# The first batch in quarters, and two PSUM banks in one tile

## The chip, the cores and the metric

The kernel runs on one core of one Trainium2 chip. Its engines are TensorE (PE; its weight loads are listed as PEld), VectorE (DVE), ScalarE (ACT), GpSimd (POOL) and SyncE (SP), each with a queue of its own that is worked off in order. The metric is the device time of one execution in microseconds (us).

## The reference

For each of 8 batches and 8 heads, 576 queries of 64 elements attend to 72 keys and values, each the mean of 8 neighbouring rows. The attention's output, as 4608 tokens of 512 elements, goes through four experts, whose outputs are summed with weights from `domain_probs`.

```python
k_p = k.reshape(B, H, Sp, pool, D).mean(axis=3)      # Sp = 72, pool = 8
v_p = v.reshape(B, H, Sp, pool, D).mean(axis=3)
attn = softmax(scale * q @ k_p.transpose(0, 1, 3, 2))
x = (attn @ v_p).transpose(0, 2, 1, 3).reshape(B * S, H * D)
p = domain_probs / (domain_probs.sum(-1, keepdims=True) + 1e-09)
for e in range(E):                                   # E = 4
    h = np.maximum(x @ w1[e], 0.0)                   # 512 -> 1024
    out += p[:, e:e + 1] * (h @ w2[e])               # 1024 -> 512
```

## The kernel before

**Work and order.** Tokens are worked in nine chunks of 512: chunk c below 8 holds the first 512 queries of batch c, chunk 8 the 64 that remain of each batch. All arithmetic on matrices is in bf16 with sums in f32. The instructions stand on every engine in the order in which the Python code calls them; nothing is rescheduled. The framework adds the semaphore waits: it works out, from the tiles that an instruction reads and writes, which earlier instructions it has to wait for.

**The loop.** From chunk 1 on, an expert's two matrix products are each done as seven block products (a Strassen form: sums of blocks of the weights, of x and of the hidden values replace an eighth product). A step `g` of the loop issues one up product of unit 0 (step `i`), one of unit 1 (the step before) and one down product of the expert before (`down`, line 766), so an expert takes seven steps and the 32 experts of chunks 1 to 8 take 224. In each step, TensorE does 4 + 4 + 8 matmuls of 256 columns.

- An up product (`up_product`, L698) goes to a bank of its unit, and ScalarE or VectorE reads it: a copy in step 0 (L711), copies to `partial` in steps 2 and 3 (L713), relus on ScalarE in steps 1 and 5 (L715, L719), relu sums on VectorE in steps 4 and 6 (L678).
- A down product goes to one of the two `o_ps` banks, in turns. After step 0 ScalarE copies it to the other bank (L774). Otherwise it is added into `acc` in two halves: by VectorE (`add`, L845), by ScalarE where an expert 0 writes first (L843), or by ScalarE and GpSimd together in step 4 (L778, L780).
- VectorE also makes four sums of hidden values for an expert (`hidden_sums`, L250), the sums of x (`x_sum`), and `weight_sums` in the first steps of the loop.
- The attention of the next batch is put between the steps, by slots of a plan (28 steps for a batch). Scores of two pairs are issued in one slot by `scores_of_two`: the first pair into `att`, the second into the second banks of both units; ScalarE's exponentials (L399, L413) read them. In the step after it, the two up products are issued in reverse. Contexts (L463) are divided on VectorE (L424, L425), and turned by DMA transposes on SP's queue, as keys and queries are.

**PSUM.** There are eight banks of 512 f32 columns. `att` is one tile of two banks. Unit 1 has two tiles of one bank, `o_ps` has two tiles of one bank, and the last two banks belong to `att_first` in the first batch, then to unit 0 as two tiles.

```python
units = [None, [psum.tile([P, NT], F32, name=f"unit1{i}") for i in range(2)]]
chains = [psum.tile([P, NT], F32, name=f"o_ps{i}") for i in range(2)]
```

**Chunk 0** is done before the loop, up to 65.2 us. `attention_first` does the attention of batch 0 and most of expert 0's up products, while the weights are still loading. Keys and values are pooled by matmuls: `sum_pool` (L314) multiplies the raw rows by a 0/1 matrix `takes`, two heads at a time; the pooled keys are copied twice side by side (L323), and turned by TensorE (`keys`, L304 and L306). Scores (L543) and exponentials (L547) run in four pieces: head group 0 or 1 by token half 0 or 1. Contexts then run by 128 tokens, the first of them in two halves of the heads (`context_half`, L437; `turn_half`, L452), the others whole (L463, L481), and `up_first` (L634) issues up products of 128 columns between them, with relus at L640. The rest of expert 0 follows in `up` (L617, relu at L622).

`first_chunk` then does plain up products of expert 1, block products of experts 2 and 3, the seven down steps of expert 0, and `down_plain` (L792: eight matmuls of 512 columns, added by VectorE at L845) for experts 1 and 2, four times each, in alternate `o_ps` banks. The attention of batch 1 is put between them: its folds (L275, L293), its queries (L371, L374), keys, scores and contexts. At the end, `down_last` (L825) does the last expert's down products in the banks of both units and of `o_ps`.

Of the kernel before, what the change touches and what calls it, by code (L numbers as in the profile page):

```python
# [12 lines left out]
BF16 = mybir.dt.bfloat16  # L13
# [4 lines left out]
def kernel(  # L18
# [44 lines left out]


    att = psum.tile([P, 2, NT], F32, name="att")
    units = [None, [psum.tile([P, NT], F32, name=f"unit1{i}") for i in range(2)]]
    chains = [psum.tile([P, NT], F32, name=f"o_ps{i}") for i in range(2)]
    psum_first = tc.tile_pool(name="psum_first", bufs=1, space=bass.MemoryType.PSUM)
    att_first = [att, psum_first.__enter__().tile([P, 2, NT], F32, name="att_first")]

# [224 lines left out]
    def keys(b, hs):  # L295
        state[("kpT", b)] = kpTs[b % 3]
        if b >= BUSY:
            nc.sync.dma_start_transpose(
                out=state[("kpT", b)][:, 0:H], in_=kp_all[:].rearrange("j h a d -> j (h a d)")
            )  # L300
            return
        kpt_ps = (chains[1][:] if b else spare_bank()).bitcast(BF16)[:, 0:H * SP].rearrange("p (h j) -> p h j", j=SP)
        for h in range(hs.start, hs.stop):
            nc.tensor.transpose(kpt_ps[:, h, :], kp_all[0:SP, h], ident[:SP, :SP])  # L304
        copy = nc.scalar.copy if b else nc.vector.tensor_copy
        copy(out=state[("kpT", b)][:, hs, 0:SP], in_=kpt_ps[:, hs])  # L306

    def sum_pool(nm, g, banks):
        n = 2 * D
# [7 lines left out]
            h = 4 * g + 2 * half  # L317
            yield slice(h, h + 2), banks[half].rearrange("j (h d) -> j h d", d=D)

    def sum_keys(g, banks):  # L320
        copies = (nc.scalar.copy if g else nc.vector.tensor_copy, nc.scalar.copy)
        for copy, (hs, kp) in zip(copies, sum_pool("kraw", g, banks), strict=True):
            copy(out=kp_all[0:SP, hs], in_=kp.unsqueeze(2).to_broadcast([SP, 2, 2, D]))  # L323

    def sum_values(g, banks):
        for hs, vp in sum_pool("vraw", g, banks):
            nc.vector.tensor_copy(out=vps[0][:, hs, 0:D], in_=vp)

    def idle(n, w_ps=None, cols=NT):

# [96 lines left out]
            in1=inv.unsqueeze(3).to_broadcast([P, n, NPAIR, D]), op=ALU.mult,  # L427
        )

    def context_half(r, g, bank):  # L430

        if g == 0:
            state[("x", 0, r)] = npool.tile([P, 2, NPAIR, D], BF16, name="x_tok", bufs=4)
        c_ps = bank.rearrange("p (a n) -> p a n", a=1)
        for i in range(NPAIR):
            at = i * (D + 1)
            nc.tensor.matmul(  # L437
                c_ps[:, 0, at:at + D + 1],
                lhsT=state[("expT", 0)][:, g * NPAIR + i, r // 2, r % 2, :],
                rhs=vps[0][:, g * NPAIR + i, :], skip_group_check=True,  # L440
            )
        divide(c_ps, state[("x", 0, r)][:, g:g + 1])

    def turn_half(r, g, bank):
        if ("xT", 0) not in state:
            state[("xT", 0)] = xpool.tile([P, KC, NT], BF16, name="xT")
        x_tok = state[("x", 0, r)][:].rearrange("p a h d -> p (a h d)")
        ks = slice(g * HK, (g + 1) * HK)
        xt_ps = bank.bitcast(BF16)[:, 0:HK * P].rearrange("p (k t) -> p k t", t=P)
        for i in range(HK):  # L450
            kc = g * HK + i
            nc.tensor.transpose(xt_ps[:, i, :], x_tok[:, kc * P:(kc + 1) * P], ident[:])  # L452
        copy = nc.scalar.copy if g else nc.vector.tensor_copy
        copy(out=state[("xT", 0)][:, ks, r * P:(r + 1) * P], in_=xt_ps)

    def context(b, r, c_ps=None):
        expT, vp = state[("expT", b)], vps[b % 3]
# [13 lines left out]
    def turn(b, r):  # L471
        if ("xT", b) not in state:
            state[("xT", b)] = xpool.tile([P, KC, NT], BF16, name="xT")
        x_tok = state.pop(("x", b, r))[:].rearrange("p a h d -> p (a h d)")
        dst = state[("xT", b)][:, :, r * P:(r + 1) * P]
        if b >= BUSY:
            nc.sync.dma_start_transpose(out=dst, in_=x_tok)
            return
        xt_ps = (units[1][0][:] if b else att_first[1][:, 0] if r == 3 else chains[0][:]).bitcast(BF16)[:, 0:KC * P].rearrange("p (k t) -> p k t", t=P)
        for kc in range(KC):  # L480
            nc.tensor.transpose(xt_ps[:, kc, :], x_tok[:, kc * P:(kc + 1) * P], ident[:])  # L481
        copy = nc.vector.tensor_copy if b == 0 and r == 3 else nc.scalar.copy
        copy(out=dst, in_=xt_ps)

    def rem_queries(i):
        qTr = apool.tile([P, NPAIR, 2, REM], BF16, name="qTr")
# [65 lines left out]
    def attention_first():  # L552

        lo, hi = groups(0)
        first, second, third, fourth = (slice(r * P, (r + 1) * P) for r in range(NR))
        half = slice(HN, NT)
        idle(13)
        rows_chosen(0)
        round_q(0)
        round_q(1)  # L560
        rows_chosen(1)
        queries(0, 0)
        queries(0, 1)
        idle(1)
        queries(0, 2)
        queries(0, 3)
        work, (B2, A2) = units[1], att_first
        work = [work[0][:], work[1][:]]
        sum_keys(0, work)
        idle(3, A2[:, 0], P)  # L570
        sum_keys(1, [B2[:, 0], B2[:, 1]])
        keys(0, lo)
        scores_first(0, 0, A2)
        keys(0, hi)
        sum_values(0, work)
        scores_first(1, 0, B2)
        context_half(0, 0, chains[1][:])
        scores_first(0, 1, A2)
        sum_values(1, work)
        turn_half(0, 0, chains[1][:])  # L580
        scores_first(1, 1, B2)
        context_half(0, 1, chains[0][:])
        context(0, 1, A2)
        up_first(range(0, 2), first, range(0, HK))
        turn_half(0, 1, chains[0][:])
        context(0, 2, B2)
        up_first(range(2, 4), first, range(0, HK))
        turn(0, 1)
        up_first(range(0, 4), first, range(HK, KC))
        context(0, 3, A2)  # L590
        turn(0, 2)
        up_first(range(0, 4), second)
        turn(0, 3)
        up_first(range(0, 4), third)
        up_first(range(0, 4), fourth)
        up_first(range(4, FCH), first)
        up_first(range(4, FCH), second)
        up(0, 0, range(4, FCH), half)

# [20 lines left out]
            nc.scalar.activation(  # L622
                out=dst, in_=out_ps.rearrange("p (t n) -> p t n", n=HN), func=ACT.Relu)

    def up_first(fcs, at, kcs=range(KC)):

        xT, H_sb = x_of(0), hidden[(0, 0)]
        for fc in fcs[::2]:
            if kcs.start == 0:
                state[("up", fc)] = (units[1] + chains[1:])[turn_of("up", 3)][:, 0:2 * P]  # L630
            out_ps = state[("up", fc)]
            for i in range(2):
                for kc in kcs:
                    nc.tensor.matmul(  # L634
                        out_ps[:, i * P:(i + 1) * P],
                        lhsT=w1_bf[:, 0, kc, (fc + i) * P:(fc + i + 1) * P], rhs=xT[:, kc, at],
                        start=(i == 0 and kc == 0), stop=(kc == KC - 1), skip_group_check=True,
                    )
            if kcs.stop == KC:
                nc.scalar.activation(  # L640
                    out=H_sb[:, fc // HF, at.start // HN, fc % HF:fc % HF + 2, at.start % HN:at.start % HN + P],
                    in_=out_ps.rearrange("p (i n) -> p i n", n=P), func=ACT.Relu)

    def weight_parts(e):
        w = w1_bf[:, e]
# [321 lines left out]
    def pieces_later():  # L967
# [17 lines left out]
            q=6, k=(5, 8, 11, 14), v=(13, 16, 19, 26), x=(24, 25, 25, 25), rem=(0, 7, 8, 14),  # L985
        )
        plans[B] = dict(usual, x=(24, 24, 25, 25), rem=(-3, 17, 21, 22))
        plans[BUSY + 1] = dict(usual, keys=-8, values=4, v=(5, 8, 12, 16))

        for b, plan in plans.items():  # L990
            start = 7 * E * (b - BUSY)
# [11 lines left out]
            if b < B:  # L1003
                put(start + plan["queries"], lambda b=b: queries(b))
                put(start + plan["keys"], lambda b=b: fold_keys(b))
                put(start + plan["keys"] + (b > BUSY), lambda b=b: keys(b, every))
                put(start + plan["values"], *values_folds(b))
                pair = 0
                for slot, n in plan["scores"]:
                    if n == 2:  # L1010
                        put(start + slot, lambda b=b, pair=pair: scores_of_two(b, pair))
                        put_amid(start + slot + 1, lambda b=b, pair=pair: scores(b, pair, 1))
                    else:
                        put(start + slot, lambda b=b, pair=pair: scores(b, pair))
                    pair += n

                for r, slot in zip((2, 3, 0, 1), plan["contexts"]):
                    put(start + slot, lambda b=b, r=r: context(b, r))
                    put(start + slot + 1, lambda b=b, r=r: turn(b, r))
# [13 lines left out]
    with tc.manual_schedule(  # L1033
# [29 lines left out]
        later, amid = pieces_later()  # L1063
        below_of = [(0, 3)] + order
        sums = {}
        for at, pieces in (((3,), weight_sums(3)[3:]), ((10, 11, 11, 12), weight_sums(1)), ((10, 15, 22, 14), weight_sums(2))):
            for slot, piece in zip(at, pieces, strict=True):
                sums.setdefault(slot, []).append(piece)
        POOLED = (4,)
# [55 lines left out]
```

## Time and profile before

| | |
|---|---|
| median of 3 runs | 489.67 us (489.37 to 489.85) |
| the profiled execution | 489.64 us, of which the span from first to last instruction is 487.80 |
| TensorE busy | 480.9 us (99% of the span) |
| VectorE, ScalarE, GpSimd busy | 378.3, 305.6, 120.7 us |
| TensorE clock granted | full in every slice |
| first plain up product of expert 1 | 23.23 us |
| first up product of the loop | 65.26 us |

The page's first part gives the busy time of each engine, the second divides the span into 40 slices, and the fourth follows the chain of work that ended last back from the end: what stands in it set the time, what does not was hidden. In a timeline, a line gives the start and the duration of one or more instructions of a kind, the engine, the source line, output and input tiles; a bracket at the end tells how long the engine had been idle and what it waited for. Matmuls are pipelined: eight of 256 columns that "took 1.04" give way to the next one 0.87 after their start.

### The profile page before, as it was taken

The numbers are of one execution on the slowest core, as the hardware profiler recorded it, in microseconds if no ns is written. First come the engines' busy times: TensorE is split into PE (matmuls) and PEld (weight loads), VectorE is DVE, ScalarE is ACT, GpSimd is POOL, SyncE is SP. The second block draws the span as 40 slices with busy tenths as digits, with TensorE's granted clock in tenths as the row PEclk, the third lists the DMA queues.
The fourth block names the chain that finished last, engine by engine and source line by source line (L and its number), as shares of the span: only waits on it lengthen the run. The fifth ranks groups of instructions, "written<-read, shape, count | busy, mean of one in ns | idle before, by whom it ended". The sixth has DMA issues, their size and how long they took to land.

```text
span 487.8 us, 11611 instructions
## 1 busy us (share of the span) xinstructions
PE 480.9 (99%) x4717; PEld 412.3 (85%) x4721; DVE 378.3 (78%) x763; ACT 305.6 (63%) x584; POOL 120.7 (25%) x121
## 2 busy tenths in 40 slices
PE   8999999999999999999999999999999999999996
PEld 4868578898889888888889889888888888888885
DVE  5789799899768976797679866997678766876674
ACT  5887446855676567656765567556765566556650
POOL 8440504243523154016411352111011101010000
PEclk9999999999999999999999999999999999999999
DMA  9999999886876789345945297311112010004003
GB/s 200 207 209 203 203 183 142 98 90 52 99 113 58 88 88 134 36 82 55 163 49 90 26 159 73 69 23 65 36 23 23 23 66 3 12 23 86 1 1 88
DMA packets 102981, 41.98 MB, mean 86 GB/s; under 512 B 73984, under 2 KB 102400, under 8 KB 102928
## 3 DMA queue, kind: packets, MB, share of 16 engines
q0 software_dynamic: 58064, 22.42, 41.0%
q1 hardware_dynamic: 43744, 17.77, 17.3%
q10 hardware_dynamic: 1120, 1.05, 0.6%
q8 instruction: 37, 0.61, 0.5%
q14 instruction: 16, 0.13, 0.1%
HBM read 45.69 MB, written 9.44 MB: 113 GB/s over the span
## 4 chain that ended last, share of the span: by engine, by line
PE 95%; POOL 1%; DMA 1%; ACT 1%; issue 0%; DVE 0%; POOLq 0%
PE unit L698 42%; PE o_ps L766 41%; PE o_ps L792 3%; PE att L463 2%; DMA w_bf<-in_moe_w_dram 1%; PE unit L825 1%; POOL wt_bf L144 1%; PE o_ps L617 1%; PE att L388 1%; PE unit L617 1%; PE unit L634 1%; PE unit L388 1%; ACT qT L374 0%; PE o_ps L634 0%; PE att L517 0%; PE att L500 0%
## 5 line engine op out<-in xcount | busy, mean ns | idle before, releaser
L845 DVE SCALAR_TENSOR_TENSOR acc<-o_ps,p_all,acc 128x256 f32<-128x256 f32 (+1 forms) x285 | 127.0, 486 | 51.5 <-PE o_ps L766 36.0
L766 PEld LDWEIGHTS <-H 128*128 128x128 bf16 x1320 | 129.1, 98 | 15.1
L698 PEld LDWEIGHTS <-w_bf 128*128 128x128 bf16 x1088 | 105.2, 98 | 13.4 <-issue 0.6
L678 DVE CUSTOM_DVE_ANT_0 H<-unit,partial 128x512 bf16<-128x512 f32 x128 | 87.3, 685 | 24.8 <-PE unit L698 10.9
L766 PE MATMUL o_ps<-w_bf,H 128*128 128x256 bf16 x792 | 102.6, 273 | 0.0
L698 PE MATMUL unit<-xT,w_bf 128*128 128x256 bf16 x704 | 100.4, 273 | 0.0
L780 POOL TENSOR_TENSOR acc<-acc,addend 128x512 f32<-128x512 f32 x24 | 30.7, 1277 | 252.3 <-ACT addend L778 211.7
L713 ACT COPY partial<-unit 128x512 f32<-128x512 f32 x128 | 72.3, 592 | 30.3 <-PE unit L698 30.2
L698 PEld LDWEIGHTS <-wu_bf 128*128 128x128 bf16 x816 | 77.6, 98 | 11.6 <-issue 2.5
L698 PE MATMUL unit<-xs,wu_bf 128*128 128x256 bf16 x512 | 77.0, 273 | 0.0
L766 PE MATMUL o_ps<-wt_bf,H 128*128 128x256 bf16 x528 | 68.4, 273 | 0.0
L715 ACT ACTIVATE H<-unit 128x512 bf16<-128x512 f32 x66 | 39.9, 605 | 30.7 <-PE unit L698 30.7
L766 PEld LDWEIGHTS <-S 128*128 128x128 bf16 x528 | 51.7, 98 | 6.0
L719 ACT ACTIVATE H<-unit 128x512 bf16<-128x512 f32 x66 | 39.6, 602 | 25.6 <-PE unit L698 25.3
L711 ACT COPY unit<-unit 128x512 f32<-128x512 f32 x68 | 39.3, 581 | 25.1 <-PE unit L698 18.6
L698 PE MATMUL unit<-xs,w_bf 128*128 128x256 bf16 x256 | 38.4, 273 | 0.0
L154 POOL DMA_DIRECT2D kraw<-in_k_dram x20 | 26.4, 1320 | 39.6 <-DMA kraw<-in_k_dram 39.6
L843 ACT ACTIVATE acc<-o_ps,p_all 128x256 f32<-128x256 f32 x72 | 30.7, 485 | 8.8 <-PE o_ps L766 7.2
L698 PE MATMUL unit<-xT,wu_bf 128*128 128x256 bf16 x240 | 35.7, 272 | 0.0
L766 PE MATMUL o_ps<-w_bf,S 128*128 128x256 bf16 x264 | 34.2, 273 | 0.0
L766 PE MATMUL o_ps<-wt_bf,S 128*128 128x256 bf16 x264 | 34.2, 273 | 0.0
L154 POOL DMA_DIRECT2D vraw<-in_v_dram x20 | 28.6, 1430 | 20.1 <-DMA vraw<-in_v_dram 20.1
(157 smaller groups left out, 508.9 us busy)
## 6 DMA issues: line engine op xcount, KB each, us to landing
out_dram<-acc SPq DMA_DIRECT2D x32, 256.0 KB, 4.3
w_bf<-in_moe_w_dram POOLq DMA_DIRECT2D x11, 512.0 KB, 12.8
q_sb<-in_q_dram POOLq DMA_DIRECT2D x7, 512.0 KB, 10.0
vraw<-in_v_dram POOLq DMA_DIRECT2D x22, 144.0 KB, 6.5
kraw<-in_k_dram POOLq DMA_DIRECT2D x21, 144.0 KB, 5.7
w_bf<-in_moe_w_dram POOLq DMA_DIRECT2D x2, 1024.0 KB, 13.9
wt_bf<-in_k_dram POOLq DMA_DIRECT2D x4, 144.0 KB, 5.4
wt_bf<-in_v_dram POOLq DMA_DIRECT2D x4, 144.0 KB, 4.1
```

Of the source, the lines that this page charges most:

```text
L154: nc.gpsimd.dma_start(out=raw[:], in_=rows_of(src, b, 2 * part, 2 * part + 2), accum_op=ALU.add if part else ALU.bypass)
L678: nc.vector._custom_dve(TENSOR_ADD_SAT, out=dst, in0=ps, in1=part, s0=LARGEST, s1=0.0)
L698: nc.tensor.matmul(ps[:, n * HN:(n + 1) * HN], lhsT=lhs[:, kc, f:f + P], rhs=rhs[:, kc, :], start=(not grows and n == 0 and kc == 0), stop ...
L711: nc.scalar.copy(out=banks[1][:], in_=ps)
L713: nc.scalar.copy(out=part[:, step - 2], in_=ps)
L715: nc.scalar.activation(out=quarter(0, 0), in_=ps, func=ACT.Relu)
L719: nc.scalar.activation(out=quarter(0, 1), in_=ps, func=ACT.Relu)
L766: nc.tensor.matmul(ps[:, j], lhsT=lhs[:, i, j * P:(j + 1) * P], rhs=rhs[:, i, :], start=(not grows and i == 0 and j == 0), stop=(i == HF - 1),
L780: nc.gpsimd.tensor_add(out=dst, in0=dst, in1=addend[:])
L792: nc.tensor.matmul(o_ps, lhsT=lhs, rhs=w2_bf[:, e, fc, :], start=(fc == 0), stop=(fc == FCH - 1), skip_group_check=True,)
L843: nc.scalar.activation(out=dst, in_=o_ps, func=ACT.Copy, scale=prob)
L845: nc.vector.scalar_tensor_tensor(out=dst, in0=o_ps, scalar=prob, in1=dst, op0=ALU.mult, op1=ALU.add,)
```

## The change

- `unit1` becomes one tile of two banks, and `o_ps` too; `units[1][i]` and `chains[i]` are now views of one bank in them. All other code uses the views as before.
- `sum_keys` makes the pooled keys in turned form: the raw rows are now the stationary operand and `takes` the moving one, one head at a time (36 matmuls of 72 columns for a group of four heads, in place of 18 of 128 columns and four turnings). One copy that spans both banks then writes four heads, and a second one writes the lower half of the rows of `kpT`.
- Contexts, turnings and up products of batch 0 run in quarters: four heads by 256 tokens (`context_quarter`, `turn_quarter`, `up_quarter`, with matmuls of 256 columns). The second half of expert 0's up products is then done over all 512 tokens in four products.
- The order of `attention_first` is rewritten around that; the other values are copied by ScalarE in part.
- In the plan of batch 3, the turning of the keys moves from slot -7 to slot -6; two of the four weight sums of expert 1 move by one step each.

```diff
-    units = [None, [psum.tile([P, NT], F32, name=f"unit1{i}") for i in range(2)]]
-    chains = [psum.tile([P, NT], F32, name=f"o_ps{i}") for i in range(2)]
+    unit_banks = psum.tile([P, 2, NT], F32, name="unit1")
+    units = [None, [unit_banks[:, i] for i in range(2)]]
+    chain_banks = psum.tile([P, 2, NT], F32, name="o_ps")
+    chains = [chain_banks[:, i] for i in range(2)]
...
-    def sum_keys(g, banks):
-        copies = (nc.scalar.copy if g else nc.vector.tensor_copy, nc.scalar.copy)
-        for copy, (hs, kp) in zip(copies, sum_pool("kraw", g, banks), strict=True):
-            copy(out=kp_all[0:SP, hs], in_=kp.unsqueeze(2).to_broadcast([SP, 2, 2, D]))
+    def sum_keys(g, banks, copies):
+        for r in range(ROWS):
+            for hh in range(2):
+                for half in range(2):
+                    ps = slice(half * PR, (half + 1) * PR)
+                    nc.tensor.matmul(
+                        banks[0:D, half, hh * SP:(hh + 1) * SP], lhsT=raws[("kraw", 0)][ps, g, hh, r, :],
+                        rhs=takes[ps, r], start=(r == hh == 0), stop=(r == ROWS - 1), skip_group_check=True,
+                    )
+        kpT = state[("kpT", 0)] = kpTs[0]
+        for dup, copy in enumerate(copies):
+            copy(out=kpT[dup * D:(dup + 1) * D, 4 * g:4 * g + 4, 0:SP].rearrange("p (b h) j -> p b h j", b=2),
+                 in_=banks[0:D, :, 0:2 * SP].rearrange("p b (h j) -> p b h j", j=SP))
...
+    def up_quarter(t, g, banks, pairs=range(2)):
         xT, H_sb = x_of(0), hidden[(0, 0)]
+        at = slice(t * HN, (t + 1) * HN)
+        for pair in pairs:
             for i in range(2):
+                f = (2 * pair + i) * P
+                for kc in range(g * HK, (g + 1) * HK):
                     nc.tensor.matmul(
+                        banks[pair][:, i * HN:(i + 1) * HN], lhsT=w1_bf[:, 0, kc, f:f + P], rhs=xT[:, kc, at],
+                        start=(i == kc == 0), stop=(kc == KC - 1), skip_group_check=True,
                     )
+            if g:
                 nc.scalar.activation(
+                    out=H_sb[:, 0, t, 2 * pair:2 * pair + 2, :].rearrange("p i n -> p (i n)"),
+                    in_=banks[pair], func=ACT.Relu)
...
+        (B2, A2), C2 = att_first, chain_banks
+        work, tail = [bank[:] for bank in units[1]], chains
+        vector, scalar = nc.vector.tensor_copy, nc.scalar.copy
+        sum_keys(0, unit_banks, (vector, scalar))
+        idle(3, B2[:, 0], P)
         scores_first(0, 0, A2)
+        sum_keys(1, unit_banks, (vector, vector))
+        scores_first(0, 1, B2)
+        scores_first(1, 0, A2)
+        sum_values(0, work, (vector, vector))
         scores_first(1, 1, B2)
+        context_quarter(0, 0, C2)
+        context_quarter(1, 0, A2)
+        sum_values(1, work, (vector, scalar))
+        turn_quarter(0, 0, tail[1], scalar)
+        turn_quarter(1, 0, A2[:, 0], scalar)
+        up_quarter(0, 0, tail, (0,))
+        context_quarter(0, 1, B2)
+        up_quarter(0, 0, tail, (1,))
+        up_quarter(1, 0, work, (0,))
+        context_quarter(1, 1, A2)
+        up_quarter(1, 0, work, (1,))
+        turn_quarter(0, 1, B2[:, 0], scalar)
+        up_quarter(0, 1, tail)
+        turn_quarter(1, 1, A2[:, 0], scalar)
+        up_quarter(1, 1, work)
+        for fc, bank in enumerate((tail + work), HF):
+            up(0, 0, (fc,), bank=bank)
...
-        plans[BUSY + 1] = dict(usual, keys=-8, values=4, v=(5, 8, 12, 16))
+        plans[BUSY + 1] = dict(usual, keys=-8, turned=-6, values=4, v=(5, 8, 12, 16))
...
-        for at, pieces in (((3,), weight_sums(3)[3:]), ((10, 11, 11, 12), weight_sums(1)), ((10, 15, 22, 14), weight_sums(2))):
+        for at, pieces in (((3,), weight_sums(3)[3:]), ((10, 10, 11, 11), weight_sums(1)), ((10, 15, 22, 14), weight_sums(2))):
```

## The prediction

> **What bounds the kernel now.** I read the page's busy table and clock row first, then its chain, then the timeline of a steady stretch, then of the front.
>
> ```profile
> PE 480.9 (99%) x4717; PEld 412.3 (85%) x4721; DVE 378.3 (78%) x763; ACT 305.6 (63%) x584; POOL 120.7 (25%) x121
> PEclk9999999999999999999999999999999999999999
> PE 95%; POOL 1%; DMA 1%; ACT 1%; issue 0%; DVE 0%; POOLq 0%
> PE unit L698 42%; PE o_ps L766 41%; PE o_ps L792 3%; PE att L463 2%; DMA w_bf<-in_moe_w_dram 1%; PE unit L825 1%; POOL wt_bf L144 1%; PE o_ps L617 1%; PE att L388 1%; PE unit L617 1%; PE unit L634 1%; PE unit L388 1%; ACT qT L374 0%; PE o_ps L634 0%; PE att L517 0%; PE att L500 0%
> ```
>
> TensorE is the bound and hardly ever waits: 95% of the chain is its matmuls, at full clock. So a stall of TensorE is paid in full, and what other engines save is worth nothing. The next view is the timeline of the loop: start, duration, engine, line.
>
> ```profile
> 266.66 0.60 PE L698 MATMUL unit<-xs,wu_bf 128*128 128x256 bf16 x4
> 267.10 1.04 PE L766 MATMUL o_ps<-wt_bf,S 128*128 128x256 bf16 x8
> 267.97 0.60 PE L698 MATMUL unit<-xs,wu_bf 128*128 128x256 bf16 x4
> 268.17 0.88 DVE L845 SCALAR_TENSOR_TENSOR acc<-o_ps,p_all,acc 128x256 f32<-128x256 f32 x2 [0.20 <-PE o_ps L766]
> 268.41 0.60 PE L698 MATMUL unit<-xT,w_bf 128*128 128x256 bf16 x4
> 268.85 1.04 PE L766 MATMUL o_ps<-wt_bf,H 128*128 128x256 bf16 x8
> ...
> 271.73 0.84 ACT L778 ACTIVATE addend<-o_ps,p_all 128x256 f32<-128x256 f32 x2 [0.77 <-PE o_ps L766]
> ```
>
> A step is two up products (0.44 each) and one down product (267.10 to 267.97: 0.87), 1.75 us. The two adds that read the down product start 0.20 after it (0.27 elsewhere) and end at 269.05. The next down product starts at 268.85, before that: it writes the other o_ps bank. The kernel lives on this overlap.
>
> **The waits, the main term.** The change makes one tile of the two o_ps banks, and one of the two banks of unit 1. I followed the semaphore waits of both built programs back to the instruction that each names. Before, all 197 waits of a matmul for a reader of o_ps name a reader of the bank it will write. After, 205 of 240 name a reader of the other bank; so do 175 of the 259 on unit 1. Each down product must now wait until the previous one is read out. Queued behind that wait are all later matmuls.
>
> The price of a step: adds end 0.20 to 0.27 (take 0.235) + 0.87 after the product; restart of TensorE 0.06 (below: 9.68 + 0.31 to 10.05); together 1.16, of which the up products cover 0.87: a stall of 0.29. Where ScalarE reads (0.84), 0.20 + 0.84 + 0.06 - 0.87 = 0.22. After down step 0 it is 0.20 + 0.57 (the L774 copy) + 0.06 < 0.87: none. After down step 6 the adds also stand behind a hidden sum and a relu sum (0.68 each, L250 and L678) that were queued after the adds of step 5: I get 0.33. An expert of seven down steps: 4 x 0.29 + 0.22 + 0.33 = 1.71; an expert 0, whose steps 1, 2, 3 and 6 are read by ScalarE, 4 x 0.22 + 2 x 0.29 = 1.46. The loop has 24 and 8 of them: 41.0 + 11.7 = **52.7**.
>
> **Scores in the loop.** In five of six batches at slot 2, in all six at slot 9, scores go to the second banks of both units. The next step is issued in reverse, unit 1 first, into the other bank; now it waits for the second exponential.
>
> ```profile
> 291.65 0.38 PE L388 MATMUL unit<-qT,kpT 64*128 64x256 bf16 x4
> 291.97 0.61 PE L698 MATMUL unit<-xs,wu_bf 128*128 128x256 bf16 x4
> 292.31 1.07 ACT L413 ACTIVATE expT<-unit 72x512 bf16<-72x512 f32 x2
> ```
>
> 0.20 + 1.07 + 0.06 = 1.33, against 0.29 already counted: +1.05. At slot 9 ScalarE's own adds (0.84) stand before the exponentials: about +1.5, and the third exponential (1.05) then delays the adds of the next step: +0.8. Sum 5 x 1.05 + 6 x 2.3 = **19.1**.
>
> **Fillers and extra VectorE work.** Contexts, remainders and turns between two down products fill part of a stall that I counted (0.35 of work against 0.29): some 12 places x 0.29, **-3.5**. VectorE work that stands before the adds (weight sums and wide folds of the first loop batch, 0.68 each, and three x sums at one slot) was free and now is late for the next product: perhaps a third of 14 us, **+4.5**; ends 0 and 14.
>
> **First chunk after the first batch** (23.2 to 65.2 before). Eight plain down products alternate the banks with nothing between them in places:
>
> ```profile
> 52.83 3.63 PE L792 MATMUL o_ps<-w_bf,H 128*128 128x512 bf16 x16
> 55.09 0.74 DVE L845 SCALAR_TENSOR_TENSOR acc<-o_ps,p_all,acc 128x512 f32<-128x512 f32 x1
> ```
>
> Each handover now costs 0.20 + 0.75 + 0.06 = 1.0 less what lies between (0.35 to 0.6): 4.4 over eight. Expert 1's up products that hit the other bank of unit 1 wait 0.85 twice (ScalarE's 0.60 relu): 1.7. The seven down steps of expert 0: 1.7, and at step 6 the folds of the second batch (44.02 to 46.67 before) hold up the adds that it now waits for: 3.1. Unit 1 and the key and query turnings in o_ps: 2.0. Sum **12.9**.
>
> **First batch.** Its matmul work stays: 96 x 0.057 + 16 x 0.109 = 7.2 us of up products become 32 x 0.109 + 16 x 0.217 = 7.0. Keys pooled in turned form drop eight turnings and a copy, but need 36 small matmuls for 18.
>
> ```profile
> 7.55 0.42 DVE L361 COPY qT<-o_ps 128x512 bf16<-128x512 bf16 x1
> 9.68 0.31 DVE L306 COPY kpT<-o_ps 128x288 bf16<-128x288 bf16 x1 [0.94 <-PE o_ps L304]
> 10.05 0.40 PE L543 MATMUL att_first<-qT,kpT 64*128 64x128 bf16 x8 [0.40 <-DVE kpT L306]
> ```
>
> The second query turning waits for the 7.55 copy in the other o_ps bank (to 8.02); 36 matmuls at 0.03 (18 LDWEIGHTS took 0.54) and two key copies in a row (0.45 each, one engine after the other, both read unit 1) put the first scores at 11.2 instead of 10.05. The 72-wide matmul is not in the trace: from 0.03 to the 0.057 of a 128-wide one, 1.1 to 2.1; I take 1.1, as its weights are the smaller ones. The second scores read the head beside them, so they wait for the second key group: the second exponential moves from 11.59 to 14.1, and the four end 2.5 later. Then the copies of the turned x delay the first up quarter by 1.0, and six relu or copy handovers inside the two merged tiles cost 0.85 to 1.2 each, 5.5. Sum **9.0**. The down of the last expert adds one handover, **1.1**.
>
> **Edits with no price.** The turning of keys goes one step later behind a turning of x in SP's queue: 1.8 us of DMA with eight steps (14 us) before the scores that need it. The two weight sums that go a step earlier are 0.68 of VectorE work each, needed three steps later; without that cover 1.4 in all.
>
> **The sum.** 52.7 + 19.1 - 3.5 + 4.5 + 12.9 + 9.0 + 1.1 = 95.8. The profiled execution took 489.64 (span 487.80 and 1.84 around it), 0.03 below the median, so 585.4, about 585.
>
> **Two rules of the Trainium skill.** The trace has two adds reading one o_ps bank (268.17 to 269.05) while a product is written into the other (from 268.85): banks are independent. "PSUM — Partial Sum Buffer" (PSUM bank collisions) tells one to guard by bank and quadrant; by it the new waits need not exist and the sum would be that of the second rival. But the built program has them, and the chip runs the program. And the granted clock is 1.00 even from 5.5 to 10.0 us, where TensorE was busy 3.64 of 4.50. "TensorE: Matmul & The Clock Gate" (A second HAM failure mode) warns that small idle gaps between matmul groups, from cycling PSUM banks, can bring back the half clock; by an estimate from it, a loop (224 steps of 1.75, 391 us) of which a quarter ran so would pay 98 more.
>
> **Rivals.**
>
> Stalls smaller than the steps say: the loop is elastic, and only the front and the plain downs pay. Against it: 1.16 of readout cannot fit under 0.87. It would give 489.6 + 22 + 5 to 30, 515 to 542: chance 0.08.
>
> Faster: the other-bank waits have always been met when they are reached, and the front gains what TensorE idled there. The windows of the front (length, then busy time of each engine, the granted clock before the DMA share):
>
> ```profile
> 5.50:10.00 4.50, 3.64 (x62) 2.52 (x60) 2.97 (x7) 3.23 (x7) 4.50 (x8) 1.00 1.21 204
> 10.00:16.90 6.90, 6.34 (x136) 5.16 (x137) 4.51 (x15) 5.58 (x9) 5.28 (x8) 1.00 1.23 203
> ```
>
> 4.50 - 3.64 + 6.90 - 6.34 = 1.4, so 488.2. It decides only if readout with both latencies stays under 0.87; the shortest reader of a down step that adds is 0.84 by itself. Chance 0.02; with no net effect, 0.01.
>
> Much slower: waits chain over engines, each late add delaying the hidden sums and these the next product. If a further 0.68 stood before the adds in half of the 192 steps that stall, 65 more: 650. For it: VectorE is 78% busy with work in fixed order. Against: the longer steps give it slack (9.8 us of work per expert in 14 instead of 12.2). Chance 0.09.
>
> The forecast: 0.80.
>
> **How the numbers follow.** Low end: half of the front (11), 38 in the loop (0.20 latency, every filler used), 9 for scores, -4, 0 and 1: 545. High end: front 28, 0.4 per step (76), 27, -2, 10, 1: 628. About 0.2% (1 us) is what a measurement can tell from no change. Slower 0.97, within 0.01, faster 0.02.
>
> **What would show it.** The page after should list TensorE idle before o_ps L769 and unit 1, released by VectorE and ScalarE, some 70 us in all, where before there was none; steps of about 2.0 us instead of 1.75; VectorE's idle before its adds on o_ps grown; the clock row unchanged; the first up product of expert 1 near 32 instead of 23. I am wrong if down products still start 1.75 apart in the loop.

## The result, and the profile after

The changed kernel takes **579.38 us** (median of 6 runs, 576.48 to 580.33) against 489.70 us before (6 runs, 489.37 to 490.52): ratio **1.1813**, 95% interval 1.1791 to 1.1836. The profiled execution took 576.6 us, its span is 574.8. The two executions with a mean granted clock of 1.00, the profiled one among them, took 576.5 and 576.6 us, the four with 0.988 to 0.991 took 579.3 to 580.3.

First the page of the changed kernel: the row of busy times, the granted clock, and the two rows of the chain of waits.

```profile
PE 510.3 (89%) x4680; PEld 409.9 (71%) x4685; DVE 379.6 (66%) x758; ACT 306.9 (53%) x576; POOL 120.4 (21%) x121
PEclk9999999999999999999999999999999999999999
PE 15%; DVE 8%; ACT 3%; issue 2%; DVEq 0%; ACTq 0%
PE o_ps L769 11%; DVE acc L848 6%; PE unit L701 2%; ACT acc L846 1%; PE unit L828 1%; DVE H L681 1%; ACT addend L781 1%; DVE S L252 0%; ACT H L718 0%; ACT o_ps L777 0%; DVE xs L252 0%; PE att L473 0%; PE o_ps L828 0%; ACT partial L716 0%; DVEq L848 0%
```

VectorE, ScalarE and GpSimd do the work they did before, to 1.3 us each. TensorE was idle 6.9 us of its span (487.8 - 480.9) and is now idle 64.5 (574.8 - 510.3). The other 29.4 us of the 87.0 stand in its busy time although the matmuls behind the first batch are the same: a group of eight shows 1.04 us when nothing follows it and occupies 0.87 when the next one does, so a stall also uncovers a tail of 0.17. The chain no longer runs along TensorE: it passes from the down product (L769) to the add that reads it (VectorE, L848) and back. (Its shares end at 28%; further back the listing does not follow it.)

The timeline of the loop, TensorE and VectorE in turns (start, duration, engine, line; in brackets the idle time before it and who ended it):

```profile
320.83 1.03 PE L769 MATMUL o_ps<-wt_bf,S 128*128 128x256 bf16 x8 [0.16 <-DVE acc L848]
321.70 0.60 PE L701 MATMUL unit<-xs,wu_bf 128*128 128x256 bf16 x4
321.90 0.88 DVE L848 SCALAR_TENSOR_TENSOR acc<-o_ps,p_all,acc 128x256 f32<-128x256 f32 x2 [0.53 <-PE o_ps L769]
322.14 0.60 PE L701 MATMUL unit<-xT,w_bf 128*128 128x256 bf16 x4
322.83 1.03 PE L769 MATMUL o_ps<-wt_bf,H 128*128 128x256 bf16 x8
...
326.11 0.84 ACT L781 ACTIVATE addend<-o_ps,p_all 128x256 f32<-128x256 f32 x2 [1.17 <-PE o_ps L769]
```

The down product ends at 321.70, the adds start 0.20 later, end at 322.78, and 0.05 after that the next down product starts. Two up products fill 0.87 of the 1.13. Before, such a step took 1.75 us and the adds ended after the next product had begun; now it takes 2.00. The starts that follow are 2.07, 2.10, 2.07, 2.00 and 1.74 apart: the last is the step after the copy, which has no stall. The last line is ScalarE's read-out within the step of 2.10; the down product that it reads gave way at 325.77.

The groups of instructions (busy time, mean ns of one, then idle time of the engine before them): VectorE now waits 98.5 us before its adds where it waited 51.5, and the weight loads of the down products on `H` stand idle for 52.8 us, 38.1 of it "issue", where it was 15.1. Two rows of before, then the same two after:

```profile
L845 DVE SCALAR_TENSOR_TENSOR acc<-o_ps,p_all,acc 128x256 f32<-128x256 f32 (+1 forms) x285 | 127.0, 486 | 51.5 <-PE o_ps L766 36.0
L766 PEld LDWEIGHTS <-H 128*128 128x128 bf16 x1320 | 129.1, 98 | 15.1
L848 DVE SCALAR_TENSOR_TENSOR acc<-o_ps,p_all,acc 128x256 f32<-128x256 f32 (+1 forms) x285 | 127.3, 487 | 98.5 <-PE o_ps L769 77.9
L769 PEld LDWEIGHTS <-H 128*128 128x128 bf16 x1320 | 128.3, 97 | 52.8 <-issue 38.1
```

The step of the loop after scores of heads, where unit 1 waits for an exponential in its other bank:

```profile
334.01 0.38 PE L399 MATMUL unit<-qT,kpT 64*128 64x256 bf16 x4
334.43 1.07 ACT L424 ACTIVATE expT<-unit 72x512 bf16<-72x512 f32 x2 [0.71 <-PE unit L399]
335.55 0.60 PE L701 MATMUL unit<-xs,wu_bf 128*128 128x256 bf16 x4 [1.16 <-ACT expT L424]
```

And the first batch, TensorE alone: the second turning of queries, two handovers at the up products, and the first up product of expert 1.

```profile
8.06 0.38 PE L368 MATMUL o_ps<-ident,q_sb 128*128 128x128 bf16 x4 [1.50 <-DVE qT L372]
...
24.29 0.60 PE L638 MATMUL unit<-xT,w_bf 128*128 128x256 bf16 x4 [0.94 <-ACT xT L463]
25.57 0.60 PE L638 MATMUL unit<-xT,w_bf 128*128 128x256 bf16 x4 [0.69 <-ACT H L643]
...
32.00 1.02 PE L622 MATMUL unit<-xT,w_bf 128*128 128x512 bf16 x4 [0.69 <-ACT H L627]
```

**A ruler for all runs.** Four places can be found in every timeline: the first up product of expert 1 (before: at 23.23), the up product of the loop's first step (65.26), the first down product of the last expert (476.71), and the end of the span (487.80). The table gives how much later each stretch between them became, in the profiled execution of each kernel, us. Spans are listed to 0.1 us, so the last column is good to 0.1.

| kernel | median us | ratio, 95% interval | first batch | first chunk | loop | end |
|---|---|---|---|---|---|---|
| changed | 579.38 | 1.1791 to 1.1836 | +8.77 | +11.35 | +65.66 | +1.22 |
| before, both tiles merged | 575.11 | 1.1721 to 1.1788 | +6.25 | +11.34 | +66.02 | +1.19 |
| before, o_ps merged | 556.35 | 1.1341 to 1.1381 | +2.37 | +8.53 | +55.04 | +0.06 |
| before, unit 1 merged | 523.11 | 1.0664 to 1.0699 | +3.85 | +2.89 | +25.17 | +1.19 |
| changed, merged in the first batch only | 500.26 | 1.0196 to 1.0227 | +10.53 | -0.01 | -0.43 | +0.01 |
| changed, one-bank tiles | 492.55 | 1.0045 to 1.0069 | +3.26 | -0.01 | -0.43 | -0.02 |
| that, last third reordered | 489.83 | 0.9991 to 1.0008 | +0.33 | 0.00 | -0.43 | 0.00 |

### The profile page after: what moved, and what is told of

It is laid out like the page before. It is cut to its first block, busy times and chain, and to the rows that moved or that the text cites. A ratio compares the mean times of both kernels' runs of the same rounds, so it can differ in the third digit from the quotient of the medians.

```text
span 574.8 us, 11601 instructions
## 1 busy us (share of the span) xinstructions
PE 510.3 (89%) x4680; PEld 409.9 (71%) x4685; DVE 379.6 (66%) x758; ACT 306.9 (53%) x576; POOL 120.4 (21%) x121
## 3 DMA queue, kind: packets, MB, share of 16 engines
q10 hardware_dynamic: 1120, 1.05, 0.5%
## 5 line engine op out<-in xcount | busy, mean ns | idle before, releaser
L848 DVE SCALAR_TENSOR_TENSOR acc<-o_ps,p_all,acc 128x256 f32<-128x256 f32 (+1 forms) x285 | 127.3, 487 | 98.5 <-PE o_ps L769 77.9
L769 PEld LDWEIGHTS <-H 128*128 128x128 bf16 x1320 | 128.3, 97 | 52.8 <-issue 38.1
L701 PEld LDWEIGHTS <-w_bf 128*128 128x128 bf16 x1088 | 105.2, 98 | 14.3 <-issue 1.6
L769 PE MATMUL o_ps<-w_bf,H 128*128 128x256 bf16 x792 | 102.5, 272 | 6.0 <-DVE acc L848 2.2
L701 PE MATMUL unit<-xT,w_bf 128*128 128x256 bf16 x704 | 100.6, 272 | 1.1 <-DVE partial L681 0.9
L701 PEld LDWEIGHTS <-wu_bf 128*128 128x128 bf16 x816 | 78.3, 98 | 29.5 <-issue 19.8
L701 PE MATMUL unit<-xs,wu_bf 128*128 128x256 bf16 x512 | 76.8, 273 | 14.2 <-ACT expT L424 14.2
L769 PE MATMUL o_ps<-wt_bf,H 128*128 128x256 bf16 x528 | 68.2, 272 | 13.7 <-DVE acc L848 6.3
L769 PEld LDWEIGHTS <-S 128*128 128x128 bf16 x528 | 51.3, 97 | 19.9 <-issue 14.1
L701 PE MATMUL unit<-xs,w_bf 128*128 128x256 bf16 x256 | 38.4, 273 | 0.0
L769 PE MATMUL o_ps<-w_bf,S 128*128 128x256 bf16 x264 | 34.1, 272 | 3.5 <-DVE acc L848 2.9
L701 PE MATMUL unit<-xT,wu_bf 128*128 128x256 bf16 x240 | 35.6, 272 | 1.8 <-DVE H L681 1.0
L769 PE MATMUL o_ps<-wt_bf,S 128*128 128x256 bf16 x264 | 34.1, 272 | 3.1 <-DVE acc L848 2.1
L781 ACT ACTIVATE addend<-o_ps,p_all 128x256 f32<-128x256 f32 x48 | 20.1, 470 | 26.1 <-PE o_ps L769 23.4
```

The source lines that it names most:

```text
L701: nc.tensor.matmul(ps[:, n * HN:(n + 1) * HN], lhsT=lhs[:, kc, f:f + P], rhs=rhs[:, kc, :], start=(not grows and n == 0 and kc == 0), stop ...
L769: nc.tensor.matmul(ps[:, j], lhsT=lhs[:, i, j * P:(j + 1) * P], rhs=rhs[:, i, :], start=(not grows and i == 0 and j == 0), stop=(i == HF - 1),
L781: nc.scalar.activation(out=addend[:, j], in_=ps[:, j], func=ACT.Copy, scale=prob)
L848: nc.vector.scalar_tensor_tensor(out=dst, in0=o_ps, scalar=prob, in1=dst, op0=ALU.mult, op1=ALU.add,)
```

## Experiments: which part of the change costs

**Both tiles merged, nothing else.** To the kernel before:

```diff
-    units = [None, [psum.tile([P, NT], F32, name=f"unit1{i}") for i in range(2)]]
-    chains = [psum.tile([P, NT], F32, name=f"o_ps{i}") for i in range(2)]
+    unit_banks = psum.tile([P, 2, NT], F32, name="unit1")
+    units = [None, [unit_banks[:, i] for i in range(2)]]
+    chain_banks = psum.tile([P, 2, NT], F32, name="o_ps")
+    chains = [chain_banks[:, i] for i in range(2)]
```

> The kernel before, with nothing changed but the two declarations: one two-bank tile for o_ps and one for unit 1. 207 of the 244 waits of a matmul for a reader of o_ps now name the other bank, as after the change. Theory (waits between the banks of one tile): the loop and the first chunk lose what they lose after the change, 65.7 and 11.4 us by the profile after, and the old first batch some 2 to 6 at its own handovers: 489.7 + 79 to 83, so 569 to 573. Rival (the new first batch and the moved steps do it): within 1 us of 489.7. Rival (half and half, the new first batch delaying everything behind it): about 530.

Measured 575.11, 2.1 above the theory's range: 85.4 us more, by two declarations. The loop and the first chunk lose within 0.4 us what they lose after the change. The old first batch lost more (6.25) than the 2 to 6 expected. The new batch and the moved steps are not what costs the 66 us.

**One tile merged at a time** (the first two or the last two lines of that diff).

> The kernel before with one two-bank tile for o_ps alone; unit 1 keeps two tiles. Theory: the terms on o_ps, 52.7 for the steps of the loop, 3.5 less for fillers, up to 4.5 for late VectorE work, about 10 of the first chunk, 1 at the end: 489.7 + 60 to 65, so 550 to 555. Rival (stalls of the loop are elastic and only the scores on unit 1 pay): 500 to 505.

Measured 556.35, 1.4 us above the range, and over 50 from the rival. The o_ps tile alone makes 55.0 of the loop.

> The kernel before with one two-bank tile for unit 1 alone; o_ps keeps two tiles. Theory: only the score steps and some up products of the first chunk and first batch wait for the other bank. The record had 19.1 us for the scores and 1.7 to 3.7 for the first chunk; the profile after shows 14.2 us of waits of unit 1 for exponentials. So 489.7 + 14 to 23, 504 to 513, and this with the run of o_ps alone should add up to the run with both within 5 us. Rival (the waits on unit 1 are always met when reached): within 1 us of 489.7.

Measured 523.11: a miss, 10 us above the range; and the two runs add up to 100.0 us (66.6 + 33.4) where both together cost 85.4. The list of waits of the unit 1 run (engine, line, waited for: us in all, times, longest), from 70 to 510 us, shows what the theory left out:

```profile
PE unit L699 <- ACT expT L414: 14.5, 11, 1.7
PE unit L699 <- DVE H L679: 5.3, 10, 1.0
```

Behind the exponentials stand VectorE's relu sums, which read unit 1 after VectorE's adds. I compared the intervals between the 224 down products of the loop with those of before. With unit 1 merged the steps after scores become 1.21 (slot 2) and 1.44 to 1.74 (slot 9) longer, 15.1 in all; the intervals after down step 4 become longer by 6.1 and those after step 6 by 3.8, the places of the relu sums. With both tiles merged those 9.9 us vanish: after step 4 the loss is 11.0 with both and 10.9 with o_ps alone, after step 6 it is 4.9 and 4.9. The step that already waits for o_ps gives VectorE the time. And the step after slot 9 loses 1.43 with o_ps alone but 0.78 with both, 3.9 less in all, because ScalarE catches up during the stall before it. So what unit 1's tile adds to the loop of the changed kernel is 66.0 - 55.0 = 11.0 us, not 25.

**Merged tiles in the first batch only**: in the changed kernel both wide tiles are taken from the pool that is given up after the first batch, and one-bank tiles are declared in the same banks behind it.

```diff
+    psum_one = psum_first.__enter__()
-    unit_banks = psum.tile([P, 2, NT], F32, name="unit1")
+    unit_banks = psum_one.tile([P, 2, NT], F32, name="unit1")
-    chain_banks = psum.tile([P, 2, NT], F32, name="o_ps")
+    chain_banks = psum_one.tile([P, 2, NT], F32, name="o_ps")
...
+        units[1] = [psum_last.tile([P, NT], F32, name=f"unit1{i}") for i in range(2)]
+        chains[:] = [psum_last.tile([P, NT], F32, name=f"o_ps{i}") for i in range(2)]
```

> The changed kernel, but its two-bank tiles of unit 1 and o_ps live only as long as the first batch; after it both are two one-bank tiles again, in the same banks. Nine waits for another bank or for the tiles given up are left, all at the first batch and the change of tiles. Theory: the 11.4 us of the first chunk, the 65.7 of the loop and the 1.2 of the end go; of the 8.8 us of the first batch 3 to 8.8 stay: 492.5 to 498.5. Rival (the new order of the first batch and the moved steps cost the loop its time): 560 or more. Rival (the new first batch gains once nothing behind it waits): under 489.

Measured 500.26: 1.8 us above the theory's range, and 60 below the rival's. In the table the first chunk, the loop and the end are back at zero, and all 10.5 us lie in the first batch. That is 1.8 more than the changed kernel's own first batch. Of this 0.5 was there at the second query turning already (8.58 against 8.06); the lag is still 0.5 at the up quarter of 24.80 us and 1.8 at the up product of 29.48. In between lies a drop of the clock. The windows of this run (window, length, busy time of each engine, then the granted clock):

```profile
21.00:22.00 1.00, 0.33 (x5) 0.22 (x3) 0.46 (x1) 0.59 (x1) 0.24 (x1) 1.00 1.24 228
22.00:23.00 1.00, 0.35 (x4) 0.17 (x2) 0.00 (x0) 0.60 (x1) 0.00 (x0) 1.00 1.30 212
23.00:24.00 1.00, 0.82 (x8) 0.65 (x8) 0.00 (x0) 0.33 (x1) 0.74 (x1) 1.00 1.21 198
24.00:25.00 1.00, 0.20 (x2) 0.19 (x2) 0.22 (x1) 0.74 (x2) 0.00 (x0) 0.98 1.25 204
25.00:26.00 1.00, 0.67 (x4) 0.29 (x3) 0.97 (x4) 0.29 (x1) 0.65 (x1) 0.50 1.25 209
26.00:27.00 1.00, 0.64 (x4) 0.46 (x4) 0.97 (x3) 0.31 (x1) 1.00 (x2) 0.50 1.24 205
27.00:28.00 1.00, 1.00 (x4) 0.41 (x3) 0.97 (x2) 0.59 (x1) 1.00 (x3) 0.50 1.24 205
28.00:29.00 1.00, 0.80 (x3) 0.25 (x2) 0.93 (x4) 0.17 (x2) 0.59 (x1) 0.81 1.24 208
```

After four microseconds in which TensorE worked 1.70 (21 to 25 us), the clock falls to one half at 25 us and is back during the window from 28.

**The new first batch with one-bank tiles throughout** (the declarations of before; the key copies and the first division go bank by bank):

```diff
-        for dup, copy in enumerate(copies):
-            copy(out=kpT[dup * D:(dup + 1) * D, 4 * g:4 * g + 4, 0:SP].rearrange("p (b h) j -> p b h j", b=2),
-                 in_=banks[0:D, :, 0:2 * SP].rearrange("p b (h j) -> p b h j", j=SP))
+        for half in range(2):
+            for dup, copy in enumerate(copies):
+                h = 4 * g + 2 * half
+                copy(out=kpT[dup * D:(dup + 1) * D, h:h + 2, 0:SP],
+                     in_=banks[half][0:D, 0:2 * SP].rearrange("p (h j) -> p h j", j=SP))
```

> The changed kernel with one-bank tiles throughout: the key copies read one bank each (four small ones in place of two), the first context quarter is divided bank by bank, and no matmul waits for a reader of another bank any more. What is left of the change is the new first batch and the moved steps. Of the 10.5 us that the first batch cost with its two-bank tiles, five handovers of 0.69, the second query turning (0.5) and the last one at expert 1 go. Theory: the new order itself still costs, since the fourth quarter of the up products waits for the exponentials and turnings in a row: 489.7 + 4 to 7, so 494 to 497. Rival (the new first batch was meant well and gains once nothing waits): under 489. Rival (the order has no price, all of it was the tiles): within 1 us of 489.7.

Measured 492.55, +2.9, between the theory and the second rival: the new order costs a little even with no wait for another bank. Its list of waits in the first 32 us names where:

```profile
PE unit L642 <- ACT xT L467: 1.0, 1, 1.0
PE unit L626 <- ACT H L631: 0.7, 1, 0.7
PE o_ps L642 <- ACT xT L467: 0.7, 1, 0.7
PE att_first L465 <- DVE x_tok L436: 0.5, 1, 0.5
```

**That kernel with its last third reordered**, to take these four away:

```diff
-    turns = {"spare": 0, "work": 0, "att": 0, "up": 0}
+    turns = {"spare": 0, "work": 0, "att": 0, "up": 1}
...
-        sum_values(1, work, (vector, scalar))
+        sum_values(1, work, (scalar, scalar))
         turn_quarter(0, 0, tail[1], scalar)
+        context_quarter(0, 1, B2)
         turn_quarter(1, 0, A2[:, 0], scalar)
-        up_quarter(0, 0, tail, (0,))
-        context_quarter(0, 1, B2)
-        up_quarter(0, 0, tail, (1,))
-        up_quarter(1, 0, work, (0,))
-        context_quarter(1, 1, A2)
-        up_quarter(1, 0, work, (1,))
+        up_quarter(0, 0, tail)
         turn_quarter(0, 1, B2[:, 0], scalar)
-        up_quarter(0, 1, tail)
-        turn_quarter(1, 1, A2[:, 0], scalar)
+        context_quarter(1, 1, A2)
+        up_quarter(1, 0, work)
+        up_quarter(0, 1, tail, (0,))
+        turn_quarter(1, 1, A2[:, 0], vector)
+        up_quarter(0, 1, tail, (1,))
         up_quarter(1, 1, work)
```

> The kernel of the new first batch with one-bank tiles, its last third reordered: the second context quarter of each token half is issued before the turnings and up quarters that it had behind it, both last value copies go to ScalarE, the last turning's copy to VectorE, and the first up product of expert 1 goes to a bank that was released longer ago. In the profile of the kernel that it starts from, waits of 0.46, 0.67, 0.99 and 0.69 (a bank still being read, same bank) stand at these places. Theory: about 0.46 + 0.67 + 0.4 + 0.69 = 2.2 of the 2.9 us goes, so 490 to 491. Rival (the quarters are bound by their chain of exponentials, which moved nowhere): 492 to 493. A gain over the kernel before needs 0.7 more than the theory has: 488.5 to 489.4.

Measured 489.83, ratio 1.0000 (0.9991 to 1.0008), 0.2 below the theory's range: within the spread of the executions the whole 2.9 us was these waits. The first batch in quarters is then as fast as the old one, and no faster: the old one left TensorE idle for only 1.4 us from 5.5 to 16.9, by the prediction's windows.

**The other parts alone.** The moved turning (of batch 3, the fourth) and weight sums, in the kernel before:

> The kernel before with only the moved steps: the turning of the fifth batch's keys a step or more later, two weight sums of expert 1 one step earlier. Theory: within 0.5 us of 489.7. Rival (a turning delays those queued behind it, or a weight sum holds up the adds): 490.4 to 491.7.

489.53, ratio 0.9995 (0.9987 to 1.0004): nothing that can be told from no change.

The turned keys, in the old order, copied bank by bank:

> The kernel before with one part of the new first batch alone: keys of the first batch pooled in turned form (36 small matmuls in place of 18 and eight turnings), copied out bank by bank, in the old order with one-bank tiles. By the trace the first scores can start at about 9.2 in place of 10.05 and the second exponential 0.4 earlier, but TensorE idles only 1.4 us from 5.5 to 16.9. Theory: between 1.0 less and 0.3 more than 489.7. Rival (turned pooling is what costs in the new first batch): 1 to 3 more.

489.82, ratio 1.0002 (0.9994 to 1.0011): nothing that can be told from no change. The first scores started at 9.93, not 9.2, and the second ones at 11.67, still behind DVE's four copies: no gain to be had.

## Experiments: the price of a wait

**A shorter read-out in the changed kernel.**

```diff
-            for j in range(BLOCKS):
-                add(ps[:, j], c, e, row * BLOCKS + j, cols, first)
+            if e == 0 and first:
+                for j in range(BLOCKS):
+                    add(ps[:, j], c, e, row * BLOCKS + j, cols, first)
+            else:
+                dst = acc[:, row * BLOCKS:(row + 1) * BLOCKS, cols]
+                nc.vector.scalar_tensor_tensor(
+                    out=dst, in0=ps, scalar=p_all[:, c * NR + row * BLOCKS, e:e + 1], in1=dst,
+                    op0=ALU.mult, op1=ALU.add)
```

> The changed kernel, but a down product that VectorE reads is read by one add over both blocks of 256 columns, with the first block's probabilities for both, in place of two. The price formula of the record: read-out of 0.20 to 0.27 + 0.74 (the row of the 512-wide add) + 0.06, less 0.87 of cover, so 0.15 a step in place of 0.29. 112 steps of the loop and the 32 last steps of an expert: 144 x 0.14 = 20 us less, 579.4 - 20, so 556 to 563. Rival (the stall is a fixed price of two banks in one tile, whatever the reader takes): 577 to 580. Rival (the chain of late VectorE work, not the read-out): more than 30 less, since 0.14 a step also brings that work forward.

With the first block's probabilities for both blocks the sums come out wrong; the number and the shape of the products stay. Measured 560.31 (560.01 to 560.93), 19.1 less than the changed kernel; against that kernel's profiled execution at full clock it is 16.5 (574.8 - 558.3), of which 15.9 in the loop. There are 136 such steps in the loop and not 144, since an expert 0's last step is read by ScalarE: 0.12 a step. Steps that stalled for an add of 0.88 and had nothing else between them stall 0.13 less (0.33 became 0.20 after step 1, 0.32 became 0.19 after step 5), as the add of 0.75 is 0.13 shorter. The timeline shows the shorter add and the restart right behind it:

```profile
300.53 0.75 DVE L790 SCALAR_TENSOR_TENSOR acc<-o_ps,p_all,acc 128x512 f32<-128x512 f32 x1 [0.53 <-PE o_ps L769]
301.33 1.03 PE L769 MATMUL o_ps<-wt_bf,H 128*128 128x256 bf16 x8
```

300.53 + 0.75 + 0.05 = 301.33. The stall is read-out time, and follows it.

**The same edit in the kernel before.**

> The kernel before, with one-bank tiles, and the same shortened read-out as in the run of one add a step (one add over 512 columns with the first block's probabilities). Theory: with separate banks the read-out lies beside the next products, so 14% less of it is worth nothing: 489.2 to 489.9. Rival (the adds set the pace in both kernels, and the 20 us were VectorE's): 480 or less.

489.79, ratio 1.0006 (0.9997 to 1.0015). The same 0.13 us a step is worth 16 to 19 us in one kernel and nothing in the other: in one-bank tiles the read-out lies beside other products.

**Cover at the scores**, in the kernel with unit 1 merged alone:

```diff
-            for args in reversed(ups) if g in amid else ups:
+            for args in ups:
```

> The kernel of unit 1 merged alone (523.1 us), but after scores the next step issues unit 0's product first, not unit 1's. Theory (unit 1's product waits for the exponential of the other bank, with nothing ahead of it to cover it): 0.44 of each of the 11 waits of 1.21 and 1.44 is covered, 4.8 less, 517.5 to 519. Rival (the stall at scores is ScalarE's or VectorE's lateness, which any product behind it meets): 522 to 524.

Measured 518.24, 4.9 less than 523.11. One product of 0.44 ahead of the waiting one takes 0.44 off each of the 11 stalls: between down products the steps after scores are 10.3 us longer than before, where they were 15.1; a slot 9 that cost 1.44 costs 1.01. The list of waits, from 70 to 505 us:

```profile
PE unit L699 <- ACT expT L414: 8.5, 11, 1.1
```

The same 11 places had 14.5.

## Why the prediction was right

579.38 lies 5.6 us from 585.0. Its cause is shown: two declarations make 85 us (first run), without them the rest of the change costs 2.9 us (the run with one-bank tiles), and nothing once its last third is reordered, and the price of a wait follows the read-out and the cover. The nearness is in part luck: at full clock the profile shows 87.0 us where the sum had 95.8, and some 3 us of the median are a lower clock, for which the sum had no term.

By its own steps, with the ruler:

- **The down steps of the loop** (52.7, with fillers -3.5 and late work +4.5 together 53.7): 55.0 with o_ps merged alone. That these agree is luck in part: the 55.0 holds 7.3 us of scores (six steps after slot 9 that lose 1.43, where such a step loses 0.21 without scores). I compared each interval between two down products of the changed kernel with the same one before. Where nothing else stands between, an expert loses 0.00 after step 0, then 0.33, 0.26, 0.32, 0.35, 0.32 and 0.25, sum 1.83 where I had 1.71; an expert 0 loses 1.63 where I had 1.46. Over 32 experts, with an expert 1 a little lower, that is 55.6 (52.7). The largest error in it is the step after step 4: I put 0.22 for ScalarE's read-out, and it was 0.35, since ScalarE began 0.34 after the product, not 0.20 (325.77 to 326.11). Fillers take back 8.6 at some 30 places, where I had 3.5 at 12; late VectorE work adds 2.5 (4.5).
- **Scores** (19.1): 14.9. This term and the fillers are what was mis-sized. Beyond what the same step loses without scores, slot 2 costs 0.89 (1.05 expected), slot 9 1.18 (1.5), and the step after slot 9 0.56 (0.8). I had added waits of which one pays in part for the other: the step after slot 9 loses 1.43 with o_ps alone and 0.78 here, since the stall before it gives ScalarE time.
- **First chunk** (12.9): 11.35. Of the eight plain down products (4.4) seven show waits of 0.36, 0.84, 0.58, 0.36, 0.36, 0.36 and 1.00, 3.9 (the last one lies behind the ruler's mark, in the loop's 65.66); step 6 of expert 0 waits 2.7 (3.1).
- **First batch** (9.0): 8.77, the first up product of expert 1 at 32.00 where I said near 32. Inside, the small key matmuls took 0.020 each (9.04 to 9.75 for 36) and not 0.03, and the first scores came at 10.36 and 10.79, not 11.2. The handovers were 0.67 to 0.94, not 0.85 to 1.2, and there were seven, not six. By the one-bank run 3.3 of the 8.8 are the new order and 5.5 the tiles; I had put nearly all of it down to the tiles, so the total is nearer than its parts.
- **The end** (1.1): 1.2. **Edits with no price** (0): 0. (The terms of the high end of the range add up to 630, not 628.)

The view that I named for it was half right. I said TensorE would show some 70 us idle before o_ps L769 and unit 1, with a releaser. It is idle 64.5 in all, but the list of waits puts only 33 us before L769 and L701 down to exponentials and adds (engine, line, waited for: us in all, times, longest):

```profile
PE unit L701 <- ACT expT L424: 14.2, 11, 1.4
PE o_ps L769 <- DVE acc L848: 13.4, 56, 2.7
PE o_ps L769 <- ACT acc L846: 3.7, 6, 0.6
PE o_ps L769 <- ACT addend L781: 1.9, 10, 0.2
```

Much of the rest appears as "issue" before weight loads, and 29.4 as tails in the busy time. Whoever looks for such a stall looks at the distance of starts.

The rivals: elastic stalls (515 to 542) fell with the run of o_ps alone, and "faster" with the one-bank runs, which reach 489.8 at best. "Much slower" had its mechanism the wrong way round: with both tiles merged the stalls overlap, 14.6 us less than the sum of the two single runs, and do not grow.

**The rules of the Trainium skill.** On banks, "PSUM — Partial Sum Buffer" (PSUM bank collisions), to guard by bank and quadrant, agrees with the runs: with the same banks in one-bank tiles the loop's 66 us are gone. The waits came from the tile and not from the memory. On the clock, "TensorE: Matmul & The Clock Gate" (A second HAM failure mode) warned of half clock from small gaps. In the loop no trace shows it. In the first batch one trace does: 0.50 for three microseconds in the windows above. By the times of the changed kernel's executions the lower clock is worth some 3 us, not 98; where it lay in those that were not profiled, and whether gaps of this kind brought it about, no run shows. I had taken the clock row as settled.

## What to carry to other kernels

Where the framework tracks waits by tile, a PSUM tile that spans two banks that take turns takes the double buffer away; keep a tile to one bank. Giving the wide tile up after the stage that uses it saves what lies behind (500.26 in place of 579.38), but the stage itself still pays (492.55 with one-bank tiles throughout). Price such a wait as (delay to the reader + its read-out + restart - work issued between), step by step, and then ask of each pair of stalls on one path whether the first gives the second's engine the time it lacked. A reorder of a stretch that already keeps TensorE busy has little to win: here the medians of two versions of the first batch lie within 0.1 us of each other.

## What was not expected of the hardware

A stretch of four microseconds with TensorE at 43% (1.70 of 4) was followed by half clock for some three, and a very similar stretch of the changed kernel's profiled execution (1.99 of 4 from 20 to 24 us, 1.85 of 4 from 22 to 26) was not. What decides between them stays open.
